# A token's factor and its number written to its row by one copy instead of two

## The chip, the cores and the metric

The kernel runs on one core of one Trainium2 chip. The metric is device time in microseconds (us) for one execution of the whole program, as the median of several runs. The names of the engines are those of the profile: PE is the matrix engine (TensorE), PEld its weight loads, DVE the vector engine, ACT the scalar engine, POOL the GpSimd engine, and SP the queue that issues most of the transfers. Each of them takes its instructions in the order in which they stand in the program; they wait for each other and for transfers (DMA) by semaphores.

## The reference

Three layers follow each other, all in float32 on the host. The first is an attention in which keys and values are first gathered into 32 memory slots per head; the second is a dense layer with a squared relu; the third routes each of the 4608 tokens to one of 8 experts.

```python
# first layer: B=8 batches, H=8 heads, S=576, D=64, M=32
a = softmax(phi, over the sequence)
k_m, v_m = a^T k, a^T v
attn_out = softmax(q k_m^T / sqrt(D)) v_m
x = attn_out as [4608, 512]
# second layer: w_in 512x2048, w_out 2048x512
h = np.maximum(x @ w_in, 0.0)
x = h * h @ w_out
# third layer: 8 experts, w1 512x1024, w2 1024x512 each
logits = x @ w_gate
expert_idx = np.argmax(logits, axis=1)
gate_w = softmax(logits)[token, expert_idx]
for e in range(E):
    mask = expert_idx == e
    out[mask] = gate_w[mask, None] * (np.maximum(x[mask] @ w1[e], 0.0) @ w2[e])
```

## The kernel before, in words

Every large product is computed in float16 from two parts of a number, a high part and the rest, with three matmuls in place of one. The scales that this needs are powers of two.

**Start.** The weights of the second layer come in as 8-byte numbers, and DVE makes 4-byte numbers of them in three instructions for each piece (lines 258 to 260), with a first step on ACT (line 249). At the same time POOL makes the constants: a unit matrix, and, by 36 small instructions (line 151), the tile `tok`, which holds the number of the token in each row of each 128-row tile, 36 columns wide.

**Second layer.** The tokens go through in 12 groups of 384. For a group and each of 16 blocks of hidden units, PE makes `h` (line 668), ACT and DVE make `g`, its squared relu in two parts (lines 676 to 680; the last step, line 680, is DVE's), and PE adds the product with `w_out` into three `acc` banks (line 688). In between, steps of the attention for later batches and of the stream that splits the experts' weights (`weight_stream`, lines 616 to 645) are mixed in. That stream stages the weights with loads by SP (lines 597 and 599), splits them on ACT and DVE (lines 643 and 644), and stores them by SP to `ws1` and `ws2` (line 645). SP also loads q (line 354), k and v (line 345) and phi (line 336) for the attention.

**Routing.** When a group's `acc` is done, `route` runs over it in steps. It splits the token rows into the first 1024 columns of the three tiles `rec` (lines 741 on ACT and 742 on DVE), turns them for the logits, finds each token's expert and its place among that expert's rows, and forms the token's factor `dq` (line 801): the softmax weight and the scales that have to be undone. The factor (line 808) and the token's number (line 809) are copied into the last columns of `rec`, and POOL scatters the 128 rows of each `rec` tile to a buffer `scr` in device memory (line 91), ordered by expert. There are three `rec` tiles for the whole program, so group i+1 writes over what group i has scattered.

**Third layer.** Tiles of 128 rows of `scr` go through their expert's weights (lines 1021 and 1048). The factor and the number of each row are read from `scr` with the row; the factor scales the result on ACT (line 1061) and the number says to which row of the output POOL scatters it. The first four tiles are taken before the last groups have been routed; the rest is planned when all have.

**What sets the order.** The code above says what depends on what. A scheduler in the framework puts the instructions of each engine into one order, by priorities and by its own estimate of durations, and adds the waits; only SP's order in the third layer is written out by hand. A changed instruction can therefore move others.

The copy of the number and the scatter that follows it, as they stand before:

```python
V.tensor_copy(rec[tt][:, 2 * DM:2 * DM + 2].bitcast(F32), dq[:, tt:tt + 1])
V.tensor_copy(
    rec[tt][:, 2 * DM + 2:2 * DM + 4].bitcast(I32), tok[:, 3 * i + tt:3 * i + tt + 1]
)
scatter(scr, sl[:, tt:tt + 1], rec[tt][:, :], E * REG - 1, "scr")
```

Of the kernel before, what the change touches and what calls it, by code (L numbers as in the profile page):

```python
# [12 lines left out]
F32 = mybir.dt.float32  # L13
I16 = mybir.dt.int16
I32 = mybir.dt.int32
U32 = mybir.dt.uint32
AF = mybir.ActivationFunctionType
ALU = mybir.AluOpType
# [5 lines left out]
P = 128  # L24
B, H, S, D, M = 8, 8, 576, 64, 32
DM, DFF, NT, E, F = 512, 2048, 4608, 8, 1024
# [32 lines left out]
def tile_attention__then__moe__then__moe2(  # L59
# [14 lines left out]
    V, A, G, T, SP = nc.vector, nc.scalar, nc.gpsimd, nc.tensor, nc.sync  # L74
# [14 lines left out]
    def scatter(dst, index, src, bound, group):  # L89

        i = G.indirect_dma_start(  # L91
            out=dst[:, :], out_offset=bass.IndirectOffsetOnAxis(ap=index, axis=0),
            in_=src, in_offset=None, bounds_check=bound, oob_is_err=False,
        )
        tc.declare_no_dep(i.ins, group=group, reason="distinct rows")
        tc.add_to_no_dep_group(group, i.ins)
# [4 lines left out]
    def const(shape, dtype, name):  # L101
        return pm.tile(shape, dtype, name=name)
# [9 lines left out]
    e8 = const([P, 3, E], F32, "e8")  # L112
    e8m = const([P, 3, E], F32, "e8m")
    er3 = const([P, 3, E], F32, "er3")
    tok = const([P, NT // P], I32, "tok")
    iota_k = const([P, K2], I16, "iota_k")

    def make_consts_a():
# [590 lines left out]
    rec = []  # L709
# [19 lines left out]
    def route(i):  # L729
        sm = pm.tile([P, 8, 3], F32, tag="sm", name=f"sm{i}", bufs=2)  # L730
        am, t, s, gate = sm[:, 0], sm[:, 1], sm[:, 2], sm[:, 3]
# [14 lines left out]
        dq = sm[:, 4]  # L746
# [51 lines left out]
        )  # L798
        V.tensor_scalar(gate, gate, EPS, None, ALU.add)
        V.reciprocal(gate, gate)  # L800
        V.tensor_tensor(dq, dq, gate, op=ALU.mult)
        V.tensor_tensor(c, rk.rearrange("p (a e) -> p a e", a=3), er3, op=ALU.add)
        V.tensor_tensor(c, c, oh, op=ALU.mult)
        V.tensor_reduce(fi, c, axis=AX.X, op=ALU.add)
        sl = pm.tile([P, 3], I32, tag="sl", name=f"sl{i}", bufs=2)
        V.tensor_copy(sl, fi)
        for tt in range(3):
            V.tensor_copy(rec[tt][:, 2 * DM:2 * DM + 2].bitcast(F32), dq[:, tt:tt + 1])
            V.tensor_copy(
                rec[tt][:, 2 * DM + 2:2 * DM + 4].bitcast(I32), tok[:, 3 * i + tt:3 * i + tt + 1]  # L810
            )
            scatter(scr, sl[:, tt:tt + 1], rec[tt][:, :], E * REG - 1, "scr")
        yield

# [329 lines left out]
    for n in range(n_total + LAG):  # L1144
        if n < n_total:
            i, f = divmod(n, NF)
# [12 lines left out]
        if n >= LAG:  # L1159
            m = n - LAG  # L1160
            g2(m)
            if m % NF == NF - 1:
                rgen.append((m // NF, route(m // NF)))
# [146 lines left out]
```

## Time and profile before

| | |
|---|---|
| median of 3 runs | 1264.56 us (1263.05 to 1271.3) |
| profiled execution | 1263.46 us |
| its span, first to last instruction | 1261.8 us |
| PE busy | 1157.6 us (92%) |
| DVE busy | 654.6 us (52%) |
| ACT busy | 650.8 us (52%) |
| POOL busy | 116.2 us (9%) |

The span is what the trace's clock covers, from the first to the last instruction of the program; the profiled execution lasted 1.66 us longer. Times inside the trace count from the start of the span. A busy PE is one that has matmuls under way; PEclk is the clock that was granted to it, where 1.00 is 2.4 GHz and 0.50 is 1.2 GHz. The idle time in square brackets at the end of a row of the timeline is the time that the engine stood still just before that instruction, and behind the arrow stands what ended it.

### The profile page before, as it was taken

What the parts mean: (1) busy time and instruction counts of PE and PEld (TensorE: products, weight loads), DVE (VectorE), ACT (ScalarE), POOL (GpSimd) and SP (SyncE); (2) the same over time, 40 slices, a digit from 0 to 9 for tenths busy, and PEclk for the clock granted to TensorE, in tenths of its full rate; (3) what the DMA queues carried; (4) which work ended last, traced back from release to release, by engine and by line L of the source; (5) the groups of instructions that cost most, each with busy time, mean ns of one, the idle gap of its engine ahead of it and who ended that gap; (6) DMA issues with size and microseconds to landing.
All of it is one profiled execution on the core that took longest, in us unless ns stands there. A gap on an engine that the chain in (4) does not pass through costs nothing.

```text
span 1261.8 us, 20352 instructions
## 1 busy us (share of the span) xinstructions
PE 1157.6 (92%) x7306; PEld 612.8 (49%) x7306; DVE 654.6 (52%) x1687; ACT 650.8 (52%) x1315; POOL 116.2 (9%) x169
## 2 busy tenths in 40 slices
PE   2658998998999998999999999997999999999995
PEld 1325465444566555466565565543444444444442
DVE  6998886987869867766656343343111111111110
ACT  4668877796877867766656565531111111111110
POOL 1000001001010110011010100004000000000000
PEclk9769999998999998999999999999999999999998
DMA  9938389677788779673131010479557957458465
GB/s 323 319 98 218 114 205 245 186 233 221 214 240 232 231 216 274 179 204 72 26 82 27 26 35 18 122 171 279 114 102 194 261 133 193 101 142 193 101 146 144
DMA packets 310920, 209.36 MB, mean 166 GB/s; under 512 B 209311, under 2 KB 289183, under 8 KB 310816
## 3 DMA queue, kind: packets, MB, share of 16 engines
q1 hardware_dynamic: 279408, 161.70, 51.0%
q10 hardware_dynamic: 24768, 25.17, 6.4%
q0 software_dynamic: 6640, 21.16, 4.6%
q8 instruction: 59, 0.97, 0.3%
q14 instruction: 45, 0.37, 0.1%
HBM read 234.53 MB, written 55.76 MB: 230 GB/s over the span
## 4 chain that ended last, share of the span: by engine, by line
PE 53%; DMA 17%; DVE 13%; issue 9%; ACT 4%; POOL 1%; SPq 1%; POOLq 0%; ACTq 0%; DVEq 0%
PE acc L688 16%; PE e L1021 13%; PE e L1048 12%; PE h L668 8%; DMA wstage<-in_moe_w_dram 6%; DVE wo L644 2%; DMA q<-in_q_dram 2%; DMA scr<-rec,sl 1%; DMA xTb<-rec 1%; DMA gT<-g 1%; PE u L578 1%; DMA ws<-wo 1%; ACT wo L643 1%; DVE g L680 1%; PE st L482 1%
## 5 line engine op out<-in xcount | busy, mean ns | idle before, releaser
L688 PE MATMUL acc<-wo,g 128*128 128x512 f16 x1728 | 417.5, 381 | 7.9 <-DVE g L680 5.9
L688 PEld LDWEIGHTS <-g 128*128 128x128 f16 x1728 | 166.5, 99 | 179.9 <-issue 10.1
L668 PE MATMUL h<-attnT,U 128*128 128x384 f16 (+1 forms) x1536 | 230.2, 287 | 5.4 <-ACT attnT L512 2.6
L1033 DVE SCALAR_TENSOR_TENSOR g<-e,g 128x512 f16<-128x512 f32 x78 | 50.3, 686 | 306.0 <-ACT g L1032 306.0
L668 PEld LDWEIGHTS <-U 128*128 128x128 f16 x1536 | 139.5, 98 | 89.1 <-issue 18.7
L680 DVE TENSOR_TENSOR g<-r,g 128x384 f16<-128x384 f32 x192 | 105.8, 553 | 90.8 <-ACT r L679 88.4
L1021 PEld LDWEIGHTS <-xT 128*128 128x128 f16 x936 | 91.4, 98 | 121.0 <-DMA xT<-scr 8.1
L1048 PEld LDWEIGHTS <-gT 128*128 128x128 f16 x936 | 91.2, 98 | 115.6 <-DMA gT<-g 4.8
L676 ACT ACTIVATE r<-h 128x384 f32<-128x384 f32 x192 | 92.7, 484 | 74.1 <-PE h L668 64.9
L1032 ACT ACTIVATE g<-e 128x512 f16<-128x512 f32 x78 | 42.3, 594 | 169.7 <-PE e L1021 159.7
L1021 PE MATMUL e<-w,xT 128*128 128x512 f16 x528 | 119.1, 383 | 6.7 <-DMA xT<-scr 4.8
L1048 PE MATMUL e<-w,gT 128*128 128x512 f16 x528 | 117.6, 379 | 4.2 <-DMA gT<-g 3.3
L1061 ACT ACTIVATE y<-e,fac 128x512 f32<-128x512 f32 x39 | 26.8, 687 | 175.5 <-PE e L1048 169.1
L678 ACT ACTIVATE g<-r 128x384 f16<-128x384 f32 x192 | 99.7, 521 | 10.3 <-PE acc L688 6.2
L679 ACT ACTIVATE r<-r 128x384 f32<-128x384 f32 x192 | 99.5, 520 | 3.6
L1021 PE MATMUL e<-wo,xT 128*128 128x512 f16 x408 | 91.0, 379 | 1.5 <-DVE g L1033 1.4
L1048 PE MATMUL e<-wo,gT 128*128 128x512 f16 x408 | 90.9, 379 | 0.2 <-DMA gT<-g 0.2
L644 DVE SCALAR_TENSOR_TENSOR wo<-wstage,wsc,wo 128x1024 f16<-128x1024 f32 x64 | 81.1, 1278 | 18.0 <-ACT wo L643 17.4
L643 ACT ACTIVATE wo<-wstage,wsc 128x1024 f16<-128x1024 f32 x64 | 71.8, 1145 | 29.1 <-DMA ws<-wo 14.4
L91 POOL DMA_INDIRECT out_dram<-y,rt x39 | 38.0, 974 | 351.0 <-ACT y L1061 144.5
L91 POOL DMA_INDIRECT scr<-rec,sl x36 | 38.2, 1061 | 274.7 <-ACT r L676 109.2
L185 DVE TENSOR_REDUCE wm<-wstage 128x1 f32<-128x1024 f32 x32 | 38.9, 1214 | 18.4 <-DMA wstage<-in_moe_w_dram 18.4
(258 smaller groups left out, 1143.3 us busy)
## 6 DMA issues: line engine op xcount, KB each, us to landing
w<-ws ACTq DMA_DIRECT2D x36, 2048.0 KB
wo<-ws ACTq DMA_DIRECT2D x34, 2048.0 KB
wstage<-in_moe_w_dram SPq DMA_DIRECT2D x64, 512.0 KB
ws<-wo SPq DMA_DIRECT2D x64, 512.0 KB
kv<-in_k_dram SPq DMA_DIRECT2D x16, 576.0 KB
kv<-in_v_dram SPq DMA_DIRECT2D x16, 576.0 KB
q<-in_q_dram SPq DMA_DIRECT2D x64, 144.0 KB
raw_ring<-in_moe_w_out_dram SPq DMA_DIRECT2D x12, 512.0 KB
```

The source lines that it names most:

```text
L91: i = G.indirect_dma_start(out=dst[:, :], out_offset=bass.IndirectOffsetOnAxis(ap=index, axis=0), in_=src, in_offset=None, bounds_check=bo ...
L643: A.activation(hi, src, AF.Copy, scale=s)
L644: V.scalar_tensor_tensor(lo, src, s, hi, ALU.mult, ALU.subtract)
L668: T.matmul(bank[:, off:off + w], u_t[b][:, g, uh, f * P:(f + 1) * P], attnT[b][:, g, ah, s0:s0 + w], start=(x == 0), stop=(x == len(seq) - 1),
L676: A.activation(r, bank[:, 0:BLK], AF.Relu, scale=2.0 ** -10)
L678: A.activation(g[:, 0], r, AF.Square)
L679: A.activation(r, r, AF.Square)
L680: V.tensor_tensor(g[:, 1], r, g[:, 0], op=ALU.subtract)
L688: T.matmul(a, g[:, gh, tt * P:(tt + 1) * P], wo[:, f, wh, :], start=(f == 0 and x == 0), stop=(f == NF - 1 and x == 2),)
L1021: T.matmul(bank[hf], x[:, 4 * xh + c, :].bitcast(F16), w[:, c, wh * F + hf * 512:wh * F + (hf + 1) * 512], start=(c == 0 and xh == 0 and w ...
L1033: V.scalar_tensor_tensor(g[:, 1, cs], bank, 0.0, g[:, 0, cs], ALU.max, ALU.subtract)
L1048: T.matmul(a, gT[:, 8 * gh + f, :], w[:, f // 2, o:o + DM], start=(f == 0 and x == 0), stop=(f == 7 and x == 2),)
```

## The change

The tile `tok` becomes the second column of a tile `pair`, which has two 4-byte columns for each of the 36 token tiles. The product that gave `dq` is now written into the first column of `pair` for the group's three tiles. One copy of four 2-byte elements then brings the factor and the number to the end of each `rec` row, where two copies of one 4-byte element did it before.

```diff
-    tok = const([P, NT // P], I32, "tok")
+
+    pair = const([P, NT // P, 2], I32, "pair")
+    tok = pair[:, :, 1]
...
-        V.tensor_tensor(dq, dq, gate, op=ALU.mult)
+        V.tensor_tensor(pair[:, 3 * i:3 * i + 3, 0].bitcast(F32), dq, gate, op=ALU.mult)
...
         for tt in range(3):
-            V.tensor_copy(rec[tt][:, 2 * DM:2 * DM + 2].bitcast(F32), dq[:, tt:tt + 1])
-            V.tensor_copy(
-                rec[tt][:, 2 * DM + 2:2 * DM + 4].bitcast(I32), tok[:, 3 * i + tt:3 * i + tt + 1]
-            )
+            V.tensor_copy(rec[tt][:, 2 * DM:2 * DM + 4], pair[:, 3 * i + tt].bitcast(I16))
             scatter(scr, sl[:, tt:tt + 1], rec[tt][:, :], E * REG - 1, "scr")
```

The code grows by two lines near its head and shrinks by three in the loop, so that a line between them has a number two higher after the change (260 becomes 262). The rows below give, for one engine, the line, the operation, the tile written and the tiles read, with buffer numbers, and the shape written.

The first place is DVE in the start of the program, where the second layer's weights are converted (`chin`, `w_in_sb`) and the first batch's phi is summed (`ojes`). Before:

```order
L260 SCALAR_TENSOR_TENSOR w_in_sb_86<-wo_87,w_in_sb_86 128x512
L259 SCALAR_TENSOR_TENSOR w_in_sb_86<-chin2_221,w_in_sb_86 128x512
L259 SCALAR_TENSOR_TENSOR w_in_sb_86<-chin3_248,w_in_sb_86 128x512
L809 COPY rec0_768<-tok_84 128x1
L809 COPY rec1_769<-tok_84 128x1
L809 COPY rec2_770<-tok_84 128x1
L360 TENSOR_TENSOR ojes0_195<-e_t_96 128x512
L260 SCALAR_TENSOR_TENSOR w_in_sb_86<-wo_87,w_in_sb_86 128x512 x2
L160 CAST iota_k_85<-ki_148 128x39
L161 CAST cols_77<-lane_i_150 128x1
L162 CAST e8_81<-tmpi_154 128x24
L258 TENSOR_SCALAR w_in_sb_86<-chin4_273 128x512
```

Now, at the same place:

```order
L262 SCALAR_TENSOR_TENSOR w_in_sb_86<-wo_87,w_in_sb_86 128x512
L261 SCALAR_TENSOR_TENSOR w_in_sb_86<-chin2_221,w_in_sb_86 128x512
L261 SCALAR_TENSOR_TENSOR w_in_sb_86<-chin3_248,w_in_sb_86 128x512
L362 TENSOR_TENSOR ojes0_195<-e_t_96 128x512
L262 SCALAR_TENSOR_TENSOR w_in_sb_86<-wo_87,w_in_sb_86 128x512 x2
L162 CAST iota_k_85<-ki_148 128x39
L163 CAST cols_77<-lane_i_150 128x1
L164 CAST e8_81<-tmpi_154 128x24
L260 TENSOR_SCALAR w_in_sb_86<-chin4_273 128x512
```

The three copies of the number for the first group stood here, far ahead of that group's routing, because they depended on nothing but `tok` and free `rec` tiles; the copies of `pair` depend on the group's factors and no longer do.

The second place is DVE where the first group's rows have been made ready for the scatter; names of waits that end in a number of DMASW are the scatters' semaphores. Before:

```order
L808 COPY rec1_769<-sm0_1685 128x1
L806 CAST sl0_1947<-sm0_1685 128x3 [waits DVE_49]
L808 COPY rec2_770<-sm0_1685 128x1
L644 SCALAR_TENSOR_TENSOR wo16_2_3_2992<-wstage_1628,wsc2_2804,wo16_2_3_2992 128x1024 [waits DMAHW0_49,Activation_49]
L680 TENSOR_TENSOR g27_2073<-r27_2071,g27_2073 128x384 [waits Activation_49]
L360 TENSOR_TENSOR ojes3_2518<-e_t_96 128x512 [waits Activation_49]
L361 TENSOR_TENSOR ojes3_2518<-ojes3_2518,e_t_96 128x512 [waits DVE_49]
L809 COPY rec0_768<-tok_84 128x1 [waits DMASW0_49]
L362 TENSOR_TENSOR es3_2517<-ojes3_2518 128x256 [waits DVE_49]
L809 COPY rec1_769<-tok_84 128x1 [waits DMASW1_49]
L680 TENSOR_TENSOR g28_2106<-r28_2104,g28_2106 128x384 [waits Activation_49]
L680 TENSOR_TENSOR g29_2137<-r29_2135,g29_2137 128x384 [waits PE_49,Activation_49]
```

Now:

```order
L803 TENSOR_TENSOR pair_84<-sm0_1685 128x3 [waits DVE_49]
L805 TENSOR_TENSOR rc0_1895<-rc0_1895,oh16_0_100 128x24 [waits DVE_49]
L810 COPY rec0_768<-pair_84 128x4 [waits DVE_49]
L810 COPY rec1_769<-pair_84 128x4
L806 TENSOR_REDUCE sm0_1685<-rc0_1895 128x3 [waits DVE_49]
L810 COPY rec2_770<-pair_84 128x4
L182 TENSOR_SCALAR wt3_3320<-wm3_3063 128x1 [waits Pool_49]
L808 CAST sl0_1947<-sm0_1685 128x3 [waits DVE_49]
L183 TENSOR_SCALAR wsc3_3321<-wt3_3320 128x1 [waits DVE_49]
L184 TENSOR_SCALAR wt3_3320<-wt3_3320 128x1 [waits DVE_49]
L636 TENSOR_SCALAR winv_98<-wt3_3320 128x1 [waits DVE_49]
L362 TENSOR_TENSOR ojes3_2515<-e_t_96 128x512 [waits Activation_49]
```

The copies of the number for the second group stood a few rows behind the first group's scatters and waited for them, ahead of the products `g28` and `g29`; now no copy into `rec` stands there, and the next writers of `rec` are the second group's lines 743 on ACT and 744 on DVE.

The third place is SP, where k, v and phi for a batch of the attention stand among the stores and loads of the experts' weights. Before:

```order
L645 DMA ws1_73<-wo16_8_2_5786 128x4x512
L599 DMA wstage_1628<-in_moe2_w2_dram 128x2x512
L345 DMA kv0_97<-in_k_dram 96x4x384
L345 DMA kv0_97<-in_v_dram 96x4x384
L645 DMA ws1_73<-wo16_8_3_5897 128x4x512
L599 DMA wstage_1628<-in_moe2_w2_dram 128x2x512
L354 DMA q18_3611<-in_q_dram 96x6x64 x2
L354 DMA q19_3678<-in_q_dram 96x6x64 x2
```

Now:

```order
L647 DMA ws1_73<-wo16_8_2_5771 128x4x512
L601 DMA wstage_1628<-in_moe2_w2_dram 128x2x512
L647 DMA ws1_73<-wo16_8_3_5879 128x4x512
L601 DMA wstage_1628<-in_moe2_w2_dram 128x2x512
L347 DMA kv0_97<-in_k_dram 96x4x384
L347 DMA kv0_97<-in_v_dram 96x4x384
L647 DMA ws2_74<-wo16_9_0_6093 128x4x512
L599 DMA wstage_1628<-in_moe2_w1_dram 128x1024
L647 DMA ws2_74<-wo16_9_1_6168 128x4x512
L599 DMA wstage_1628<-in_moe2_w1_dram 128x1024
L356 DMA q18_3602<-in_q_dram 96x6x64 x2
```

Here k and v stand behind one more store of weights than before, and the q loads behind two more; at other places of the stream it is the same or the other way round. From the seventh group's ranking matmul (line 795) on, which starts at 588.6 us in the trace of before, PE's order is the one that it was; ahead of it some 1600 of PE's 5200 rows stand at another place. On POOL and SP the order is again that of before from about 483 us and 550 us on.

## Rows read from the trace of the kernel before

**Rows 1.** The page: granted clock in 40 slices of the span, tenths.

```profile
PEclk9769999998999998999999999999999999999998
```

**Rows 2.** Windows: length; PE, PEld, DVE, ACT, POOL busy; clock, DMA share, GB/s.

```profile
0.00:100.00 100.00, 47.23 (x316) 25.79 (x316) 87.34 (x203) 58.29 (x119) 10.94 (x55) 0.78 0.80 243
100.00:600.00 500.00, 473.69 (x3543) 275.37 (x3544) 388.77 (x959) 384.87 (x780) 43.03 (x50) 0.99 0.73 205
600.00:850.00 250.00, 248.94 (x1670) 137.83 (x1669) 117.97 (x364) 140.72 (x305) 13.96 (x15) 1.00 0.26 63
850.00:1262.00 412.00, 387.75 (x1783) 173.77 (x1781) 60.54 (x163) 66.96 (x113) 48.23 (x50) 0.99 0.67 162
```

**Rows 3.** Line 809: durations (ns), and what ended its engine's idle time.

```profile
L809 DVE COPY rec<-tok x36: 139/154/155, 22.7 to 809.4; 128x1 int32<-128x1 int32 x36
  DMA scr<-rec,sl: 33.6, 25
  POOL tok L151: 3.7, 1
```

**Rows 4.** Timeline, DVE and POOL: start, length, instruction, [idle before <-its end].

```profile
18.33 0.68 DVE L259 SCALAR_TENSOR_TENSOR w_in_sb<-chin,w_in_sb 128x512 int32<-128x512 int32 x1
20.62 2.74 POOL L151 IOTA tok<- 32x4 int32 x28
22.70 0.33 DVE L809 COPY rec<-tok 128x1 int32<-128x1 int32 x3 [3.69 <-POOL tok L151]
22.94 0.68 DVE L360 TENSOR_TENSOR ojes<-e_t 128x512 f32<-128x512 f32 x1
```

**Rows 5.** Windows, as in 2: the start behind that wait.

```profile
23.00:94.00 71.00, 38.30 (x232) 20.16 (x231) 69.63 (x165) 45.31 (x94) 5.07 (x9) 0.69 0.76 234
```

**Rows 6.** Timeline behind the first group's scatters: POOL, DVE and PE.

```profile
211.87 1.22 POOL L91 DMA_INDIRECT scr<-rec,sl  x1 [0.30 <-issue]
216.73 0.15 DVE L809 COPY rec<-tok 128x1 int32<-128x1 int32 x1 [4.49 <-DMA scr<-rec,sl]
218.11 1.69 PE L688 MATMUL acc<-wo,g 128*128 128x512 f16 x7 [2.33 <-DVE g L680]
```

**Rows 7.** Timeline: the next instruction that writes into `rec`, on ACT.

```profile
241.32 1.95 ACT L741 ACTIVATE rec<-x2f,sm 128x512 f16<-128x512 f32 x3 [0.91 <-DVE sm L737]
```

**Rows 8.** Timeline behind the second group's scatters: DVE and PE.

```profile
301.84 0.15 DVE L809 COPY rec<-tok 128x1 int32<-128x1 int32 x1 [2.75 <-DMA scr<-rec,sl]
304.46 0.15 DVE L809 COPY rec<-tok 128x1 int32<-128x1 int32 x1 [2.46 <-DMA scr<-rec,sl]
306.46 2.74 PE L688 MATMUL acc<-wo,g 128*128 128x512 f16 x6 [3.56 <-DVE g L680]
```

**Rows 9.** Windows, as in 2: the two stretches at the lower clock.

```profile
305.28:312.10 6.82, 5.38 (x18) 2.74 (x19) 6.82 (x20) 4.11 (x10) 0.46 (x1) 0.50 0.55 204
475.95:482.78 6.83, 6.83 (x32) 4.64 (x31) 2.80 (x9) 4.09 (x10) 0.14 (x1) 0.50 1.12 318
```

**Rows 10.** Timeline: a store in SP's queue, and PE after it.

```profile
468.83 4.51 SPq L645 DMA_DIRECT2D ws<-wo  x1
475.45 3.69 PE L482 MATMUL st<-kb,qT 128*96 128x64 f32 x24 [1.59 <-ACT qT L466]
```

**Rows 11.** Timeline behind the sixth group's scatters: DVE and PE.

```profile
557.39 0.15 DVE L809 COPY rec<-tok 128x1 int32<-128x1 int32 x1 [2.52 <-DMA scr<-rec,sl]
560.33 0.15 DVE L809 COPY rec<-tok 128x1 int32<-128x1 int32 x1 [2.32 <-DMA scr<-rec,sl]
559.40 2.23 PE L482 MATMUL st<-kb,qT 128*96 128x64 f32 x24
```

**Rows 12.** DVE's waits from 600 to 850 us: in total, times, longest.

```profile
DVE rec L809 <- DMA scr<-rec,sl: 13.0, 12, 1.6
```

**Rows 13.** Timeline of the last group: copies on DVE, first scatter on POOL.

```profile
844.35 0.27 DVE L808 COPY rec<-sm 128x1 f32<-128x1 f32 x3
849.33 0.97 POOL L91 DMA_INDIRECT scr<-rec,sl  x1 [41.74 <-DVE sl L806]
```

## The prediction

> **What bounds the kernel now.** I read the windows first. PE is idle for 53 of the first 100 us, for 26.3 of the 500 us up to 600 us, for 1.1 of the 250 us up to 850 us, and for 24 of the 412 us behind that [rows 2]. So from 100 us on PE's own work sets the time, and a gain can come only from the start, where DVE is the busiest engine (87 of 100 us), from PE's gaps up to 600 us, or from stretches at the lower clock. The slices of the clock [rows 1] place those: besides the start and the end there are two dips in the long row of nines, near 305 us and near 480 us. What the change touches is line 809, the copy of the number. It is short (154 ns), but DVE stood still for 33.6 us in 25 waits until a scatter had let go of the `rec` tile that it writes, and once for 3.7 us until POOL had made the numbers [rows 3]. DVE takes its instructions in order, so in these 37 us everything queued behind the copy stood still too, the products `g` that PE needs among it. The last step was to ask, wait by wait, whether PE stood still as well.
>
> **The change part by part.** The new copy reads the factor, which exists only once its group has been ranked, so it cannot stand early in DVE's order. The order of the instructions shows just that: the copies are gone from the start and from behind the scatters, and the scatter's semaphore is now waited for by the next group's lines 743 and 744.
>
> *The start.* DVE ends its work at 18.33 + 0.68 = 19.01 us, waits 3.69 us, and begins the next useful instruction 0.24 us behind the first copy [rows 4]: 3.93 us in all. From 23 to 94 us DVE is busy for 69.63 of 71 us, with the transfers at a share of 0.76 [rows 5], so it is DVE that sets the pace of the conversion, and what goes at 19 us arrives at 94 us. The ends are 0 (something else keeps DVE from starting) and 3.93; I take 3.93, because the next instructions need only what ACT has already made.
>
> POOL's numbers are still being written then, until 20.62 + 2.74 = 23.36 us, and the three copies that ran into this took 0.33 us [rows 4] against 0.27 us for three copies with POOL idle [rows 13]. The Trainium skill (SBUF — State Buffer, section Who interferes with whom) says that copies, casts and tensor_scalar instructions of DVE in a two-port mode and GpSimd's instructions shut each other out of a shared pair of ports for a whole instruction. If that held DVE off for the whole run of the iotas, this term would be 0 and the sum 3.9 us less; by the rows, a copy beside them loses some 0.02 us.
>
> *The first group's scatters.* DVE stands still for 4.49 us, up to 216.73 us, and PE, which waits for `g`, for 2.33 us [rows 6]. I take 2.33.
>
> *The second group's.* DVE stands still for 2.75 and 2.46 us, and PE for 3.56 us, up to 306.46 us [rows 8]. The clock falls at 305.28 us, inside that gap, from 1.00 to 0.50 (1.2 GHz), and is back at 312.10 us; PE is busy for 5.38 us of that stretch [rows 9], and at full clock this work takes half, so 2.69 us come on top. Together 6.25 us.
>
> *The other waits.* Behind the sixth group's scatters DVE waits 2.52 and 2.32 us, and PE works through an attention step with no idle time in its row [rows 11]: 0. Behind 600 us there are 12 waits of 13.0 us [rows 12], in a stretch where PE is idle for 1.1 us altogether: 0. What covers them is work that PE already has; were it gone, at most the 1.6 us of the longest wait would show for each group.
>
> *The wait that stays.* The scatter has to be done before the next group writes into `rec`. For the second group that is line 741 at 241.32 us [rows 7], 24.6 us behind the moment at which the first group's first scatter had let DVE go [rows 6], so nothing is queued behind an open scatter there: 0. Below 0 is excluded, above it the ends are 0 and the 4.49 us that the longest such wait took.
>
> *One copy for two.* Three copies take 0.27 us from first to last [rows 13], so 36 fewer free some 3.2 us of DVE, which has idle time in every stretch behind 100 us [rows 2]: 0. The new copy's four elements of 2 bytes have no row of their own; the copy of one 4-byte element takes 0.154 us [rows 3], a product 512 wide 0.68 us [rows 4], and I take the former, which moves as many bytes within a factor of two. At the end of the routing it would matter most, where all later tiles wait for the last group. But there the copies are done at 844.6 us and the scatter waits for `sl` until 849.33 us [rows 13]: 4.7 us of cover, 0.
>
> *The order.* With 36 instructions gone, the scheduler has also placed some 1600 of PE's first 5200 rows elsewhere, and SP's transfers with them; behind 590 us PE's order is untouched. No row prices an order that has not run. The nearest is a wait that this program does have: a store of weights held SP's queue for 4.51 us at 468.83 us, a q load stood behind it, and PE was idle for 1.59 us until q had come [rows 10]; then 6.83 us passed at the lower clock with PE busy throughout [rows 9], which cost 3.41 us. That is 5.0 us for one such wait. The ends are one such wait fewer (this one itself may go) and three more; I take one more, since a third of the rows has moved and the old order has two places of this price in 500 us.
>
> **The sum.** 3.93 + 2.33 + 6.25 = 12.51 us less, 5.0 us more: 7.5 us less. The profiled execution took 1263.46 us, 1.1 us under the median of the runs; 1263.46 - 7.5 = **1256 us**. A difference of about 1% (12.6 us, so 1251.9 and 1277.2 us as bounds) is what a measurement of this kernel can tell from none.
>
> **The rivals.**
>
> *All of it is given back (0.27).* No new wait comes: 1263.46 - 12.5 = 1251 us, and if the wait at 475 us is gone with the old order, 1246 us. For it speaks that each of the three terms has its waiting row; against it, that so many rows moved.
>
> *Other waits step in (0.22).* When DVE is free, PE meets ACT or a transfer at the same places, and only the start pays: 1259.5 us; if the start is lost to POOL's writes as well, 1263.5 us. That PE is idle for 26.3 us before 600 us, of which the two scatter gaps are 5.9, speaks for it: most of its gaps had other causes.
>
> *Slower, by SP's queue (0.08).* In the new order k and v stand behind a further store of weights, and q behind two further ones. Each store waits for the split on ACT and DVE, and everything behind it on SP waits along. If the split is late when q, k or v is wanted, PE pays 5.0 us each time, as at 475 us. The gain of 12.5 us is used up by three such waits: 1263.46 - 12.5 + 15 = 1266 us, and six would pass 1%, 1281 us. The old order has one in 500 us, which speaks against more than two or three.
>
> *The wait only moves (0.03).* If the next group's ACT and DVE writes come while the scatter is open, ACT is held in place of DVE. That needs groups closer together than the 24.6 us between [rows 6] and [rows 7]. Where it happened twice at 6.25 us, as behind the second group, the gain of 12.5 us would be used up: 1263.5 us.
>
> **How the numbers follow.** The forecast has 0.40 and, with no or two new waits in place of one, reaches from 1251 to 1261 us. The range from 1246 to 1266 us takes in all of the first two rivals and leaves out the worse half of the third and what lies beyond their ends, under 0.2. Faster by over 1% needs 1251.9 us or less: nearly all of the 0.27 and the lower edge of the forecast, 0.28. Slower by over 1% needs six new waits: 0.04. The rest, 0.68, is within 1%.
>
> **What would show it.** In the new trace no copy into `rec` may wait for a scatter or for POOL's iotas, and DVE's work at 22.94 us should begin near 19 us. PE's first matmul of `h` behind the start should come some 4 us earlier. The dip of the clock near 305 us should be missing. If PE's idle time from 100 to 600 us is still 26 us or more, the second rival is right, and the rows of SP before each gap tell whether it was the third. If line 743 or 744 waits for a scatter, the wait has only moved. The forecast is wrong if the start gains nothing, or if the order alone costs more than 10 us.

## The result, and the profile after

The changed kernel took 1281.78 us (median of 3 runs, 1281.11 to 1282.13), the kernel before 1264.56 us: a ratio of 1.0102, with a 95% interval from 1.0065 to 1.0139. The forecast was 1256 us, between 1246 and 1266. By the medians it is 17 us slower, by the ratio some 13 us, and not some 8 us faster. The profiled execution took 1281.78 us with a span of 1280.1 us, 18.3 us over the span of before.

The copies do what was said of them. The first three rows are the grouped view of line 810, which is now the only copy (durations in ns, first and last start), and of line 743, the next writer of `rec`; the two timeline rows are VectorE at the place of [rows 4].

```profile
L810 DVE COPY rec<-pair x36: 158/161/238, 217.2 to 860.7; 128x4 int16<-128x4 int16 x36
...
L743 ACT ACTIVATE rec<-x2f,sm x36: 704/707/730, 180.3 to 849.6; 128x512 f16<-128x512 f32 x36
...
  DMA scr<-rec,sl: 1.1, 1
...
18.22 1.28 DVE L261 SCALAR_TENSOR_TENSOR w_in_sb<-chin,w_in_sb 128x512 int32<-128x512 int32 x2
19.43 0.68 DVE L362 TENSOR_TENSOR ojes<-e_t 128x512 f32<-128x512 f32 x1
```

No copy waits any more, neither for a scatter nor for GpSimd, where there were 33.6 and 3.7 us [rows 3]. Line 743 waits for an open scatter once, for 1.1 us. The instruction that stood behind the three copies at 22.94 us begins at 19.43 us. So the stalls are gone, and the time went elsewhere. The clock in 40 slices, and the windows as in [rows 2]:

```profile
PEclk8668999999999999999999999999999999999998
...
0.00:100.00 100.00, 50.80 (x324) 27.09 (x324) 87.62 (x201) 58.87 (x120) 12.23 (x55) 0.73 0.83 242
100.00:600.00 500.00, 463.23 (x3418) 265.62 (x3419) 384.75 (x926) 374.84 (x761) 36.84 (x47) 0.98 0.74 204
600.00:850.00 250.00, 249.27 (x1688) 140.44 (x1686) 113.48 (x336) 146.41 (x312) 16.23 (x17) 1.00 0.22 59
850.00:1280.00 430.00, 406.24 (x1881) 181.79 (x1879) 67.28 (x189) 70.47 (x125) 48.78 (x50) 0.98 0.66 159
```

The dip near 305 us [rows 1, 9] is gone. But TensorE is idle for 36.8 us between 100 and 600 us, where it was idle for 26.3. To see where, I took from both traces the time at which TensorE starts the k-th of the 1728 products of the second projection (line 688 before, 690 now), the same work in the same sequence, and list the difference in us (k from 0):

```
product k            0     144    288    336    480    528    1056   1680
changed kernel     +4.2   +4.2  +11.8  +15.3  +13.7   +9.2  +16.7  +16.2
```

Three pieces carry it: 4.2 us are lost before the first product, 11.1 us between products 144 and 336 (168 to 249 us in the old trace), 6.1 us come back from there to product 528, where the second group's wait was [rows 8], and 7.5 us go again up to product 1056.

Not all of this is lost time, since the new order also moves TensorE's other work from one piece to another. These are the windows from product 144 to product 336, as in [rows 2], before, changed, and in the first experiment below, which runs the changed kernel in the old order:

```profile
168.17:248.49 80.32, 74.78 (x562) 45.88 (x561) 64.30 (x154) 58.49 (x117) 6.85 (x8) 1.00 0.88 230
```

```profile
172.32:263.74 91.42, 81.77 (x623) 48.18 (x621) 68.26 (x157) 64.56 (x131) 7.58 (x8) 0.98 0.82 218
```

```profile
166.02:244.61 78.59, 74.92 (x562) 45.93 (x560) 64.39 (x151) 58.45 (x118) 7.29 (x8) 1.00 0.89 235
```

TensorE runs 61 matmuls more there in the changed kernel: 50 of key-value products and their sum, 3 transposes of q and 8 of line 571 (`u`). Of the 11.1 us, 4.1 are idle time (9.65 against 5.54 us), 1.7 are the price of 3.43 us at the lower clock, and the other 5.3 are work that the old order does earlier or later. Between products 336 and 528 the changed kernel has 20 matmuls of `u` and 6 of `aT` fewer, so that part of the 6.1 us that come back is moved work too, and 12 and 6 of them more between 528 and 1056.

The start, on TensorE before, then in the changed kernel with its window behind the wait:

```profile
101.07 1.14 PE L668 MATMUL h<-attnT,U 128*128 128x384 f16 x6
103.90 1.52 PE L392 MATMUL kvm<-kv,e_t 128*32 128x128 f32 x48 [1.69 <-issue]
```

```profile
97.04 2.11 PE L670 MATMUL h<-attnT,U 128*128 128x384 f16 x12
99.21 0.66 PE L463 MATMUL qTp<-ident,q 96*128 96x96 f32 x6
104.81 2.79 PE L394 MATMUL kvm<-kv,e_t 128*32 128x128 f32 x48 [4.95 <-DMA kv<-in_v_dram]
...
103.72:113.97 10.25, 9.16 (x79) 7.45 (x80) 5.45 (x10) 1.91 (x4) 0.00 (x0) 0.50 1.09 299
```

TensorE stands still for 4.95 us until k and v have come, and then does 9.16 us of work at a granted clock of 0.50 (1.2 GHz), twice as long as at the full one. In the kernel before six `h` matmuls stood in front of these key-value products, the wait showed as 1.69 us, and the products ran at the full clock.

The second piece. These rows are the changed kernel's timeline at one of TensorE's four gaps (2.69, 1.82, 1.75 and 1.94 us) between 198 and 243 us, and its waits from 168 to 265 us (us in total, times, longest):

```profile
228.45 1.22 DVE L187 TENSOR_REDUCE wm<-wstage 128x1 f32<-128x1024 f32 x1 [4.08 <-DMA wstage<-in_moe_w_dram]
229.81 1.15 ACT L645 ACTIVATE wo<-wstage,wsc 128x1024 f16<-128x1024 f32 x1 [2.98 <-DMA ws<-wo]
231.44 0.49 ACT L678 ACTIVATE r<-h 128x384 f32<-128x384 f32 x1
231.98 0.81 PE L670 MATMUL h<-attnT,U 128*128 128x384 f16 x4 [1.75 <-ACT r L678]
...
DVE wm L187 <- DMA wstage<-in_moe_w_dram: 10.5, 5, 4.1
...
ACT wo L645 <- DMA ws<-wo: 9.9, 5, 4.3
ACT wo L618 <- DMA wstage<-in_moe_w_dram: 4.4, 3, 2.6
```

Read them from below: TensorE waits for ScalarE's `r`, and `r` stands behind the splitting of the experts' weights, which waits for a transfer of weights. The same three waits came to 4.0, 3.3 and 0.8 us in the kernel before, and to 3.7, 8.0 and 0.7 us in the first experiment, where TensorE has no such gap; so it is not their length alone, but what stands behind them. The other gaps ended otherwise. TensorE's waits from 170 to 270 us, changed, and from 165 to 260 us before:

```profile
PE qTp L463 <- issue: 2.7, 1, 2.7
PE aT L510 <- DVE pt L502: 1.9, 1, 1.9
PE rk L796 <- DVE oh L783: 1.8, 1, 1.8
PE h L670 <- ACT r L678: 1.8, 1, 1.8
```

```profile
PE rk L794 <- DVE oh L781: 2.6, 1, 2.6
PE acc L688 <- DVE g L680: 2.3, 1, 2.3
```

The wait of routing (`rk`) is there in both. New are, besides the one for `r`, the two for steps of the attention, `qTp` and `aT`. The `aT` waits for VectorE's `pt`; the `qTp` begins 0.10 us behind another `pt`, which stood behind a split of weights that had waited 3.54 us for ScalarE. Behind them lies a shift of the attention. Its sequences are counted from 0 here, as in the program: the batch that the recorded expectations call the second sequence is sequence 2, and their first is sequence 1. These rows are sequence 2's first key-value products on TensorE, before, changed, and in the first two experiments:

```profile
165.20 1.52 PE L392 MATMUL kvm<-kv,e_t 128*32 128x128 f32 x48
```

```profile
176.72 1.52 PE L394 MATMUL kvm<-kv,e_t 128*32 128x128 f32 x48
```

```profile
163.05 1.52 PE L394 MATMUL kvm<-kv,e_t 128*32 128x128 f32 x48
```

```profile
177.03 1.52 PE L392 MATMUL kvm<-kv,e_t 128*32 128x128 f32 x48
```

They open a chain of some 97 us (163.05 to 259.9 us in the first experiment, 176.72 to 274.5 us in the changed kernel, where the last `u` matmul ends), whose result the fourth group of tokens needs, from token 1152 on. TensorE does not wait for its end: the fourth group's first `h` begins without idle time at 295.4 us in the changed kernel, 12.1 us behind the last step of `U`, and at 277.6 us in the first experiment, 8.9 us behind it. What it waits for are steps inside the chain. No wait delays the start of the chain: TensorE is busy up to it, with the projection's own matmuls. In the old order 144 acc and 132 h matmuls of the program stand in front of it, in the new one 162 and 149, so 35 more. Those 35 are then missing later, as work to do beside the chain. That this is what makes the two waits for its steps is an inference from the order, which the experiments bear out in part.

### The profile page after: what moved, and what is told of

It reads as the page before. It is cut to its first block, busy times and chain, and to the rows that moved or that the text cites. A ratio compares the mean times of both kernels' runs of the same rounds, so it can differ in the third digit from the quotient of the medians.

```text
span 1280.1 us, 20330 instructions
## 1 busy us (share of the span) xinstructions
PE 1169.5 (91%) x7306; PEld 614.9 (48%) x7306; DVE 653.1 (51%) x1651; ACT 650.6 (51%) x1315; POOL 114.1 (9%) x169
## 4 chain that ended last, share of the span: by engine, by line
PE 51%; DMA 21%; DVE 10%; issue 10%; ACT 4%; SPq 2%; POOL 1%; POOLq 0%; ACTq 0%; DVEq 0%
PE acc L690 17%; PE e L1020 11%; PE e L1047 9%; PE h L670 8%; DMA wstage<-in_moe_w_dram 8%; DMA xT<-scr 2%; DVE wo L646 2%; DMA rt<-scr 2%; ACT wo L645 2%; DMA ws<-wo 2%; DMA xTb<-rec 1%; PE u L580 1%; PE kvm L394 1%; PE st L484 1%; DMA raw_ring<-in_moe_w_out_dram 1%
## 5 line engine op out<-in xcount | busy, mean ns | idle before, releaser
L682 DVE TENSOR_TENSOR g<-r,g 128x384 f16<-128x384 f32 x192 | 105.4, 552 | 114.3 <-ACT r L681 113.2
L91 POOL DMA_INDIRECT scr<-rec,sl x36 | 36.8, 1021 | 282.2 <-ACT r L678 124.1
L394 PE MATMUL kvm<-kv,e_t 128*32 128x128 f32 x768 | 36.0, 312 | 15.1 <-ACT e_t L379 6.9
```

Source lines behind the costliest of these rows:

```text
L91: i = G.indirect_dma_start(out=dst[:, :], out_offset=bass.IndirectOffsetOnAxis(ap=index, axis=0), in_=src, in_offset=None, bounds_check=bo ...
L682: V.tensor_tensor(g[:, 1], r, g[:, 0], op=ALU.subtract)
```

## The experiments

The theory after the traces was **order**: the removed waits pay what was forecast, and the order that the scheduler makes of the changed program costs more than that. The rival was **own work**: the pair copies, or VectorE's running ahead, cost it in any order. To part them I fixed the order. At the end of the program one function hangs each instruction of TensorE, VectorE and ScalarE behind the one that a table names, with an edge that sets the sequence on the engine and waits for nothing:

```diff
         tile_attention__then__moe__then__moe2(tc, *args)
+        _force(tc, nc)
...
+def _force(tc, nc):
...
+            if last is not None:
+                tc.add_manual_dep(
+                    x[k], last.name,
+                    mybir.DependencyInfo(mybir.DependencyClass.NoSync, mybir.DependencyReason.DATA),
+                    reason="order",
+                )
+            last = x[k]
```

The ratios below are to the kernel before on the same chip at the same time (its medians there were 1267 to 1275 us). "Lost between 144 and 336" is how much further product 336 lies behind the trace of before than product 144 does; it holds the moved work too.

**The changed kernel in the old order.** Edit: `_force` in the changed kernel, with the table of the kernel before.

> The changed kernel's instructions, but TensorE, VectorE and ScalarE each issue them in the order of the kernel before (the table in the file fixes it); only the number's copies are gone from VectorE's list, and GpSimd and SyncE come out in the old order too. Theory 'order' (the new order costs it, the removed waits do pay): the start's 3.69 + 0.24 us of waits are absorbed wholly or in part, the idle and low clock at 302 to 312 us go: 1251 to 1258 us. Rival 'own work' (the pair copies, their strided operand or VectorE running ahead cost it, whatever the order): 1276 to 1284. Rival 'nothing gained' (the waits only move): 1262 to 1266.

Measured: 0.9922 (0.9881 to 0.9963). The kernel before took 1272.4 us on that chip, so the expectations have to be read as ratios to 1264.56 us: 0.989 to 0.995 for "order", which holds, and 1.009 or more and 0.998 or more for the rivals, which the interval excludes. First product 2.2 us earlier than before, -1.7 us between 144 and 336, 7.8 us ahead at product 480. At the start VectorE goes on at 18.98 us:

```profile
18.98 0.68 DVE L362 TENSOR_TENSOR ojes<-e_t 128x512 f32<-128x512 f32 x1
...
100.00:600.00 500.00, 474.99 (x3549) 275.07 (x3548) 387.14 (x931) 383.83 (x775) 42.51 (x49) 0.99 0.73 205
```

The change is a gain of 0.8% when the order is left alone.

**The kernel before in the new order.** Edit: `_force` in the kernel before, with the table of the changed kernel, each number's copy behind its factor's.

> The instructions of the kernel before, two copies a tile and the numbers in their own table, but TensorE, VectorE and ScalarE issue them in the order of the changed kernel; each number's copy stands right behind its factor's copy, so it waits for no scatter either. Theory 'order': 1279 to 1285 us, as the changed kernel. Rival 'own work': 1250 to 1264, since neither the pair copy nor the strided table is there.

Measured: 1.0074 (1.0040 to 1.0108); +3.5 us at the first product and 9.4 us lost between 144 and 336. The median, 1285.0, stands against the same 1272.4 us. As ratios "order" had 1.011 to 1.016 and "own work" 0.989 to 1.000: the interval excludes the second and ends just short of the first. The new order slows the kernel before too, by less than was expected. Neither the pair copy nor its table is in this kernel; VectorE's running ahead is, but in the old order it paid. Between them the two experiments put own work out.

**Other orders by chance.**

```diff
-HP1 = 50
+HP1 = 51
```

> The changed kernel with one priority of the attention's steps (HP1) at 51 in place of 50: no work changes, the scheduler hands out another order (some 290 of VectorE's 1,635 rows stand elsewhere). Theory 'order': any value between 1250 and 1290 us, and over 3 us from the changed kernel's 1281.8 either way. Rival 'own work': within 3 us of 1281.8.

> The kernel before with HP1 at 51 in place of 50: no work changes, some 55 of VectorE's 1,677 rows stand elsewhere. Theory 'order': a few us from 1264.6 either way, which says how far an order alone moves the kernel before. Rival 'own work': within 3 us of 1264.6.

Measured: 1.0107 (1.0076 to 1.0137) and 1.0012 (0.9987 to 1.0038). Both missed what "order" expected: 290 of VectorE's rows that stand elsewhere left the changed kernel where it was, and 55 left the kernel before. So it is not any order that costs. What these two had kept was the place of sequence 2's key-value products, behind 162 and 149 and behind 144 and 132 matmuls. From this came the narrower theory, **late chain**.

**The gain, split.** Edit: `_force` in the kernel before with its own table, in which only the first group's, or only the later groups' number copies are moved behind the factor copies.

> The kernel before in its own order on every engine, but the first group's three number copies, which stand 27th to 29th on VectorE and wait for GpSimd's tables, stand behind that group's factor copies; all later number copies still wait for the scatters. Theory 'order': the start's gain alone, 1.5 to 3.9 us of the old kernel's time, ratio 0.997 to 0.999 (the old order with all copies moved began TensorE's second projection 2.2 us earlier). Rival 'the start absorbs it': 1.000 within 0.001, and the first product of that projection no earlier than 107.5 us.

> The kernel before in its own order, but the number copies of groups two to twelve stand right behind their factor copies, so that they wait for no scatter; the first group's three stay where they waited for GpSimd. Theory 'order': the scatter waits' own worth, 4 to 8.6 us (the two terms were 2.33 and 6.25), ratio 0.993 to 0.997. Rival 'other waits step in': 0 to 2 us, ratio 0.998 to 1.000.

Measured: 0.9971 (0.9947 to 0.9996) and 0.9938 (0.9911 to 0.9964), which of 1275.5 us is 3.7 and 7.9 us. One row of each: VectorE's work of 22.94 us at its earlier time, and the window where the dip near 305 us was, with the full clock.

```profile
18.61 0.68 DVE L360 TENSOR_TENSOR ojes<-e_t 128x512 f32<-128x512 f32 x1
```

```profile
298.00:310.00 12.00, 11.02 (x62) 5.76 (x61) 10.57 (x30) 7.53 (x15) 2.39 (x2) 1.00 0.96 328
```

**The loss, split by time.** Edit: `_force` in the changed kernel; up to a given product one order's table, behind it the other's.

> The changed kernel, in the old order up to the first product of the second projection (252 of TensorE's 6,667 instructions) and in the new order behind it. If the new order's 20 us are lost in places that add up, the start's 6.4 us come back and the rest stays lost: first product at 105.5 us, ratio to the kernel before 1.003 to 1.007. If only the start matters (later gaps are its echo): 0.992.

> The changed kernel, in the new order up to the 337th product of the second projection (about 264 us, 1,102 of TensorE's instructions) and in the old order behind it. If the loss lies before that place: as far behind as the changed kernel is there (19 us behind the old order's 244.6), and 17 to 21 us behind it at the end, ratio 1.006 to 1.010. If a late stream leaves more weights loaded and the old order catches up: under 1.002.

Measured: 1.0039 (1.0013 to 1.0064), first product at 107.2 us, 9.2 us lost between 144 and 336; and 1.0047 (1.0013 to 1.0081), 10.9 us lost there, of which 5.1 us came back by product 1056. The first came out as expected, but for the first product; the second lies between its two expectations, since the old order catches up in part. Both show the loss of the stretch with the new order's place of the chain, whatever stands around it.

**The old order in the middle alone.** Edit: three tables, one behind the other.

> The changed kernel: new order up to the first product of the second projection, old order from there to its 337th, new order behind. TensorE then meets the second sequence's key-value products (48 of line 394) behind 144 acc and 132 h matmuls, as in the old order, and not behind 162 and 149. Theory 'late chain' (in the new order that sequence's attention, a chain of some 97 us, starts 13.6 us later and TensorE runs out of other work inside it): the 10 us between the 144th and 337th product come back, ratio to the kernel before 0.999 to 1.004. Rival 'many small losses' (no place of its own): above 1.006.

Measured: 1.0084 (1.0058 to 1.0110). By its total this speaks for the rival. By its stretch it doesn't: from product 144 to product 288 the old middle gained 2.0 us, where the changed kernel lost 7.6. Then, at the seam to the new order, one wait took it all:

```profile
255.28 1.28 DVE L646 SCALAR_TENSOR_TENSOR wo<-wstage,wsc,wo 128x1024 f16<-128x1024 f32 x1 [4.37 <-ACT wo L645]
258.58 1.28 DVE L646 SCALAR_TENSOR_TENSOR wo<-wstage,wsc,wo 128x1024 f16<-128x1024 f32 x1 [2.02 <-ACT wo L645]
260.59 1.98 PE L571 MATMUL u<-w_in_sb,vbd 128*64 128x512 f32 x4 [9.13 <-DVE U L587]
```

VectorE's `U`, which TensorE waited for during 9.13 us, stood behind weight splits that waited in their turn. The experiment is inconclusive, since the seam is of its own making.

**Two other programs that start the chain early.**

```diff
         for tt in range(3):
+            dm = pm.tile([P, 1], I32, tag=f"dm{tt}", name=f"dm{i}_{tt}", bufs=1)
+            V.tensor_copy(dm, tok[:, 3 * i + tt:3 * i + tt + 1])
             V.tensor_copy(rec[tt][:, 2 * DM:2 * DM + 4], pair[:, 3 * i + tt].bitcast(I16))
```

> The changed kernel with 36 copies more that nobody reads: each number is also copied into a one-column tile of its own, where the number's copy once stood. It takes no wait back and adds some 36 x 0.06 us to VectorE; the scheduler's order changes with it, and the second sequence's key-value products come behind 143 acc and 129 h matmuls. Theory 'late chain': from the 144th to the 337th product it loses under 3 us against the kernel before (the changed one lost 11.1), ratio 0.992 to 1.002. Rival 'many small losses' or 'own work': 1.006 to 1.012.

```diff
-R0 = 3.0
+R0 = 4.0
```

> The changed kernel with the number of attention steps a turn of the program hands out for the second sequence (R0) at 4.0 in place of 3.0; the scheduler then puts that sequence's key-value products behind 150 acc and 144 h matmuls, where the changed kernel has 162 and 149 and the old one 144 and 132. Theory 'late chain': half or more of the 11.1 us come back in that stretch (loss of 0 to 6 us), ratio 0.994 to 1.005. Rival 'many small losses': 1.006 to 1.012.

Measured: 1.0025 (1.0005 to 1.0044) with 1.0 us lost between 144 and 336, and 0.9994 (0.9971 to 1.0017) with 1.5 us. The first total is just above what was expected, because 5.6 us went between products 0 and 48, which I did not follow up. In the stretch both did as the theory said. `R0` sets the pace of sequence 1's steps, and sequence 2 follows behind them. No copy waits in either kernel, yet both stay well short of the old order's 0.9922: an early chain is not all that an order can cost. Thirty-six copies that nobody reads make the changed kernel faster by 0.8%, by what they do to the order.

**Two late copies in the old order.** Edit: as for the split of the gain, with all number copies moved.

> The kernel before in its own order, with all 36 number copies right behind the factor copies: no copy waits, and 36 copies more than the changed kernel in the old order, from two tables. 'Copies cost nothing' (the step of the forecast): ratio 0.989 to 0.995, as the changed kernel in the old order (0.992). If fewer, wider copies matter: above 0.996.

Measured: 0.9948 (0.9926 to 0.9971), the same within the intervals as one copy in the old order. The pair copy neither pays nor costs.

**One thing late, alone.** Edit: the changed kernel with the old order's table, in which 31 of TensorE's 6667 instructions are moved; and the same with six.

> The changed kernel in the old order, with one thing moved on TensorE alone: the second sequence's key-value products, with the sum and the two q transposes that stand among them (31 instructions of the program), come behind 155 acc and 156 h matmuls, 35 matmuls later, where the new order has 162 and 149. VectorE and ScalarE keep the old order. Theory 'late chain': the old order's loss of -1.7 us from the 144th to the 337th product turns into a loss of 5 to 12 us, and the ratio to the kernel before into 0.997 to 1.002 in place of 0.992. Rival 'many small losses' (no one place of the new order matters): under 3 us lost there, ratio 0.990 to 0.995.

> The changed kernel in the old order, with one thing moved on TensorE alone: the six h matmuls that stand ahead of the first sequence's second key-value products (1.14 us at 101 us in the kernel before) come behind them and the scores, as in the new order. Theory 'the start is lost to these six': TensorE stands still for some 3.8 us in place of 1.3 to 2.7 before those products, the clock falls behind the wait for some 10 us as in the changed kernel, and the second projection begins 3 to 6 us later, at 107 to 111 us; ratio 0.995 to 0.998. Rival 'no': it begins within 1.5 us of the old order's 104.3 to 105.5, ratio 0.990 to 0.995.

Measured, the chain: 1.0105 (1.0079 to 1.0131), 6.8 us lost between 144 and 336 (8.41 us idle there, where the old order has 3.67) and 13.8 us more up to product 1056. Its key-value products, and TensorE's and VectorE's waits behind them (the three in the middle from 160 to 300 us, the last from 160 to 265 us):

```profile
170.18 1.52 PE L394 MATMUL kvm<-kv,e_t 128*32 128x128 f32 x48
...
PE h L670 <- ACT r L678: 6.9, 4, 6.1
PE acc L690 <- ACT g L680: 2.4, 1, 2.4
PE kvm L394 <- DVE U L587: 1.3, 1, 1.3
...
DVE rs L409 <- PE kvm L402: 2.8, 1, 2.8
```

Moving these 31 instructions by 35 matmuls turns the gain of 0.8% into a loss of 1.0%, more than the theory expected. But it is not the changed kernel's loss over again. VectorE and ScalarE kept the old order here, so they stood still for the late products (2.8 us on VectorE). In the stretch one wait for `r`, of 6.1 us, makes most of the idle time, and the changed kernel's two longest, for `qTp` and `aT`, are absent. Behind product 336 the 13.8 us are lost where the changed kernel loses 1.4 and the changed kernel in the old order 1.7. That the totals, 1.0105 and 1.0102, agree is chance. The experiment shows that the late chain is enough by itself to lose time in the stretch; that the changed kernel's own waits there come of it is not shown.

The six `h` matmuls: 0.9960 (0.9940 to 0.9979), and the first product at 105.4 us, as in the old order (105.5). The total lies in the theory's range, but its interval also overlaps the old order's own, so the first product has to decide. The wait grew from 1.26 to 2.69 us, less than the 3.8 expected, and the clock stayed up:

```profile
100.69 1.52 PE L394 MATMUL kvm<-kv,e_t 128*32 128x128 f32 x48 [2.69 <-DMA kv<-in_v_dram]
```

So these six alone are not what the start was lost to; that part of the theory fell.

The products' differences in us, with the place of the chain (acc and h matmuls in front of it) and TensorE's idle time between products 144 and 336 (5.5 us in the kernel before):

```
                         chain        0     144    288    336    528    1056  lost 144-336  idle
changed kernel         162, 149     +4.2   +4.2  +11.8  +15.3   +9.2  +16.7   +11.1          9.7
before, new order      162, 149     +3.5   +4.5  +10.8  +13.9  +12.1  +19.3    +9.4          7.0
changed, HP1 51        162, 149     -0.3   -1.4   +3.9   +8.9   +6.5  +12.3   +10.3          7.2
old start, new rest    162, 149     -0.5   -2.6   +3.1   +6.6   +3.1   +5.7    +9.2          6.5
new to 336, old rest   162, 149     +0.1   -1.0   +5.7   +9.9   +3.6   +4.8   +10.9          9.8
chain alone late       155, 156     +0.6   -1.4   +5.4   +5.4   +4.3  +19.2    +6.8          8.4
changed, old order     144, 132     -2.2   -2.2   -3.9   -3.9   -7.6   -2.2    -1.7          3.7
two late copies        144, 132     -3.4   -3.4   -4.6   -4.6   -8.0   -7.1    -1.2          3.3
before, HP1 51         144, 132     +2.3   +2.3   +2.1   +1.2   +1.0   +6.7    -1.1          3.7
start only             144, 132     -0.9   +0.2   +0.6   +0.6   +0.8   +4.3    +0.4          4.4
scatter waits only     144, 132     +0.6   +0.6   -1.3   -1.3   -5.8   -1.4    -1.9          3.4
six behind alone       144, 132     -2.2   -2.2   -2.8   -2.8   -6.8   -3.9    -0.6          4.0
old middle             144, 132     +4.8   +4.8   +2.8  +15.7   +7.3  +12.2   +10.9         12.4
36 idle copies         143, 129     +0.8   +6.1   +5.5   +7.1   +1.8   +8.8    +1.0          3.7
R0 4.0                 150, 144     -6.6   -5.4   -3.8   -3.9   -6.6   +0.1    +1.5          3.3
```

Every kernel with the chain late loses 7 to 11 us in that stretch. Of those with the chain early none loses more than 1.5, but for the old middle, which loses 10.9 at its seam. Moved work is in these numbers; the idle time, which is free of it, parts the same kernels, 6.5 to 9.8 us against 3.3 to 5.5. The waits for `qTp` (2.2 to 2.7 us) and `aT` (1.7 to 1.9 us) stand in all five kernels that have the new order in the stretch, and in none with the chain early are they over 0.3 us. Each row is one execution: behind the last product, where TensorE's order is the same in all, these traces still take between 430 and 442 us, so a few us in one row are not to be read alone.

## Why the prediction was wrong

**The terms of the gain were right.** The start was forecast at 3.93 us and measured at 3.7 alone (0.5 to 6.8); the two scatter waits at 2.33 + 6.25 = 8.58 us, measured at 7.9 (4.6 to 11.4). Together 12.5 forecast and 11.6 measured as the sum of the two; 9.9 (0.78% of 1272.4 us; 4.7 to 15.1) with both and the pair copy in the old order. The sign that the prediction named for the start, the first `h` some 4 us earlier, came out with the start alone moved (63.26 after 66.90 us); in the changed kernel it was 1.3 us.

**The terms at nothing were right.** The wait that stays took 1.1 us on ScalarE, once. The new copy takes 161 ns (154 were assumed), and one copy for two moved the total by less than the intervals. The prediction also asked what the start would give if the Trainium skill's rule on the shared ports (SBUF — State Buffer, section Who interferes with whom) held VectorE off for the whole run of the iotas, namely 0. That did not show: the start paid 3.7 us. Whether VectorE's instructions there ran in one of the two-port modes that the rule is about, no row tells. While GpSimd wrote its numbers in the changed kernel, a VectorE tensor_scalar took 0.41 us, the median of its line:

```profile
23.05 2.87 POOL L153 IOTA pair<- 32x4 int32 x28
23.71 0.41 DVE L260 TENSOR_SCALAR w_in_sb<-chin 128x512 int32<-128x512 int32 x1
...
L260 DVE TENSOR_SCALAR w_in_sb<-chin x16: 401/413/426, 8.4 to 40.4; 128x512 int32<-128x512 int32 x16
```

**The step that failed is "The order", at 5.0 us.** The prediction named it itself, as wrong if the order alone cost more than 10 us. It costs 1.0102 / 0.9922 = 1.018, with the two intervals combined 1.0125 to 1.0238, so some 23 us, and 1.0074 / 0.9948 = 1.013, some 16 us, with the instructions of the kernel before (1.0086 to 1.0168). I priced it as one more short wait, from the nearest row that I had, and reasoned that a third of the rows had moved. The number of moved rows says nothing: 290 of VectorE's in the one case and 55 in the other changed the time by less than could be seen, while 31 of TensorE's were enough for 1.8%. That the order costs this is shown from both sides. Where, is shown in part: the changed kernel lies 12.8 us further behind its old order at product 336 than at product 144, 6.0 of them idle time, and 6.4 us behind it at the first product. What has to be looked for is which long chain begins later. That was to be read before the run: the program's order shows 35 more matmuls in front of the chain. That VectorE and ScalarE, held by waits for weights, would then keep the chain's steps from TensorE was not to be read from it.

**The rivals.** "Other waits step in" was right in that TensorE's idle time stayed above 26 us (36.8), but its price ended at 1263.5. "Slower, by SP's queue" had the sign and a symptom. k and v do leave later, at 178.29 us where it was 166.78 us, but they wait for the key-value products that free their tile, not for a store of weights; SP's queue follows TensorE's order there. That rival got 0.08.

**What stays open.** The start. With the new order the first product came at 107.4 and 107.8 us in two kernels, and at 111.2, 111.9 and 112.4 us in the three whose clock fell for 7 to 10 us just then; with the old order there and no early copies it came at 104.3 to 108.3 us in six. The six matmuls alone do not explain it. The record has a part of the answer. The first half of sequence 1's key-value products frees the tile for the next k and v. It starts at 88.24 us both in the changed kernel (the first two rows) and in the same kernel in the old order (the other two). In the new order its last products stand behind more single transposes of q, and the load is issued 1.85 us later:

```profile
94.64 1.07 PE L394 MATMUL kvm<-kv,e_t 128*32 128x128 f32 x12
96.09 0.57 SPq L347 DMA_DIRECT2D kv<-in_k_dram  x1
```

```profile
92.78 1.06 PE L394 MATMUL kvm<-kv,e_t 128*32 128x128 f32 x10
94.24 0.57 SPq L347 DMA_DIRECT2D kv<-in_k_dram  x1
```

In all five kernels with the new order at the start the load goes out 7.85 us behind the first of these products, and 5.6 to 6.0 us behind it in the kernel before and the eight others with the old one there; no run tests this alone. The 7.5 us behind product 528 are hardly the new order's: the changed kernel in the old order loses 5.4 us there against the trace of before, and the kernel before with HP1 at 51 loses 5.7. The changed kernel has gaps of 2.67 us at 509 us and of 2.11 us at 580 us there, which were not followed up.

**A version that beats both.** The changed kernel in the old order (0.9922), or the kernel before with its number copies moved behind the factor copies and nothing else (0.9948, profiled at a span of 1251.5 us). The second is not told apart from the first by its interval. Both need the order fixed. Of the versions without a fixed order the best was R0 at 4.0, 0.9994.

## What to carry to other kernels

Where a scheduler makes the order, a change has two prices, that of its own waits and that of the new order, and the second can be the larger: compare both orders for the longest chain of dependent steps, and count how much independent work now stands in front of its first step and is missing beside it. Run the change once in the old order before you judge it; here it was a gain that its own re-ordering hid. What a removed wait pays shows in the time only as far as the new order does not take it back.

## What the runs showed of the hardware

The clock's price of a short wait varies. Behind a wait of 4.95 us the granted clock was 0.50 for 10.25 us, and 9.16 us of work took twice its time. Behind one of 2.69 us at the same place in the last experiment it did not fall, nor behind one of 2.99 us in the changed kernel with HP1 at 51; behind one of 2.22 us there, in the kernel before with HP1 at 51, it was 0.50 for 3.41 us, and the 48 key-value products took 2.79 us in place of 1.52. So the length of the one wait does not tell whether the clock falls. Behind a gap of 1.94 us at 241 us in the changed kernel it fell for 3.43 us:

```profile
243.67:247.10 3.43, 3.43 (x10) 1.18 (x8) 3.43 (x12) 3.43 (x6) 0.00 (x0) 0.50 0.00 0
```
